# K and V loads of a decode attention kernel: the 16 key runs of a head go to its 16 partitions in the opposite order

## The chip, the core and the metric

The kernel runs on one core of a Trainium2 chip. The metric is the device time of one execution in microseconds. Before the change it is 1281.42 us (median of 3 runs, 1281.33 to 1281.44).

## The reference

One decode step for 8 sequences: a layer norm, attention over a cache of 4096 keys with 32 heads of 128, and beside it a small MLP; both are added to x.

```python
B, Sq, D = 8, 1, 640
Hq, Hkv, Sk, Dh = 32, 32, 4096, 128
...
q = (x @ wq).reshape(B, Sq, Hq, Dh).transpose(0, 2, 1, 3)
scores = einsum("bhqd,bhkd->bhqk", q, k_cache) * (Dh ** -0.5)
p = softmax(scores, axis=-1)
o = einsum("bhqk,bhkd->bhqd", p, v_cache)
A = o.transpose(0, 2, 1, 3).reshape(B, Sq, Hq * Dh) @ wo
...
out = x + A(layernorm(x)) + B(layernorm(x))     # B: layernorm, w1, gelu, w2
```

All of it is in bfloat16. K and V are 268 MB each and are read once. Softmax and the sum over keys do not depend on the order of the keys, as long as K and V have the same order.

## The kernel before

The work is cut into 32 tiles (`NQ`). Tile i holds one sequence and eight heads (`HS = 8`): K of tile i is 8 heads x 4096 keys x 128 values, 8 MiB. On chip a tile lies in `S_sb` on 128 partitions with 64 KB each: head h has partitions 16h to 16h + 15, and each partition holds a run of 256 keys (`NKEY`). In HBM the 4096 keys of a head follow each other, and so do the eight heads, so a tile is 128 runs of 64 KB, one behind the other. `cache_src` (line 364) makes this view, `load_k` (368) and `load_v` (383) load with it.

`S_sb` has three slots: two for K (tiles in turn), one for V. The loads are issued by SP in one queue, in the order K(i+1), V(i), K(i+2), V(i+1). K(i) waits for the exponentials of tile i-2 (`exp`, from tile 6 on; earlier ones for its score work), which is when its slot is free; V(i) waits until PV of tile i-1 is done. V of tile 30 comes in two loads (192 and 64 of the 256 keys). Behind K31 and V30 come the MLP's weights, then V31, then wo. x and two biases are loaded by ACT, in a queue of its own.

For each tile, once K has landed (`k_ready`):

- DVE works out the scores of 176 of each partition's 256 keys in three pieces (`dve_chunk`: multiply by the query, fold, reduce in `S_sb`).
- PE transposes the other 80, ACT copies them to `KT_sb`, PE multiplies them with the query, DVE picks each partition's own head (`dve_sel`).
- DVE finds a maximum (`dve_max`), ACT takes the exponentials (`act_exp`, into `P_sb`), PE sums them over the 16 partitions of a head (`pe_RS`).
- Once V has landed PE multiplies it with `P_sb` (`pe_PV`, 256 matmuls), ACT copies the result, POOL divides by the sum.

The engines' programs are recorded in Python, sorted by hand-set places (`at(...)`) and then replayed, so nearly every instruction carries line 111 in the profile; tiles are told apart by their names.

## Time and profile before

| | |
|---|---|
| median of 3 runs | 1281.42 us |
| profiled execution, device time | 1281.24 us |
| its span, first to last instruction | 1279.9 us |
| bytes moved | 551.97 MB |
| DVE busy | 1103.0 us (86%) |
| PE busy | 672.1 us (53%) |
| ACT busy | 476.5 us (37%) |
| POOL busy | 109.6 us (9%) |

The page cuts the span into 40 equal slices: a digit is the busy share in tenths, the DMA row is the mean share of the core's 16 DMA engines, the GB/s row what they moved. "us to landing" is the time from a load's issue to its arrival, with its wait in the queue. The chain of waits follows the end of the run back, at each step to what released it.

### The profile page before, as it was taken

Reading aid. Unit: us, or ns where it says so; the run is one execution under the profiler, and the core shown is the slowest. Engines: PE = TensorE matmul, PEld = TensorE weight load, DVE = VectorE, ACT = ScalarE, POOL = GpSimd, SP = SyncE. Lnnn points to the kernel's source line nnn. Section 1 sums busy time; section 2 is a strip of 40 time slices with the busy share of each in tenths; the row PEclk is TensorE's granted clock in tenths of the full one; section 3 lists DMA queues with packets and bytes.
Section 4 is the critical chain, followed back from the end, with each engine's and each line's share of the span. In section 5 each row is a group of like instructions: output and inputs, shape, how many; then the busy total and the mean of one; then the engine's idle time right before and its main releaser. Section 6 shows DMA issues by size and latency. Waiting matters only on the chain.

```text
span 1279.9 us, 34138 instructions
## 1 busy us (share of the span) xinstructions
PE 672.1 (53%) x13794; PEld 570.6 (45%) x13794; DVE 1103.0 (86%) x684; ACT 476.5 (37%) x906; POOL 109.6 (9%) x121
## 2 busy tenths in 40 slices
PE   2536555446645446545456554456454466464476
PEld 0435444435535345444345444345343355353465
DVE  2899998889888889888899888898888898888894
ACT  0524444233444233443234443234443334442331
POOL 0020010000000000000000000000000000000050
PEclk8656655565565556555555555555565556655665
DMA  9999999999999999999999999999999999999998
GB/s 424 425 431 429 434 434 428 440 434 430 432 438 428 438 432 432 434 432 434 430 440 430 432 434 438 428 432 436 430 438 432 432 432 440 426 434 436 426 444 365
DMA packets 10784, 551.97 MB, mean 431 GB/s; under 512 B 1242, under 2 KB 1523, under 8 KB 1812
## 3 DMA queue, kind: packets, MB, share of 16 engines
q1 hardware_dynamic: 10736, 551.79, 99.7%
q8 instruction: 8, 0.13, 0.0%
q14 instruction: 4, 0.03, 0.0%
q10 hardware_dynamic: 36, 0.02, 0.0%
HBM read 551.80 MB, written 0.01 MB: 431 GB/s over the span
## 4 chain that ended last, share of the span: by engine, by line
DMA 46%; DVE 37%; issue 12%; ACT 4%; PE 1%; DVEq 0%; SPq 0%
DMA S_sb<-in_A_k_cache_dram 42%; DVE S_sb L111 26%; DVE Sd_sb L111 8%; ACT P_sb L111 4%; DMA S_sb<-in_B_w_dram 2%; DMA S_sb<-in_A_wo_dram 2%; DVE S_ps L111 1%; PE TR_ps L111 1%; DVE mx_sb L111 1%; DVE mxT_sb L111 0%; DVE mbT_sb L111 0%; DVEq L109 0%; DVE mq_sb L111 0%; DVE NB_sb L111 0%; DVE ri_sb L111 0%
## 5 line engine op out<-in xcount | busy, mean ns | idle before, releaser
L111 PE MATMUL TR_ps<-ident_bf,S_sb 128*128 128x128 bf16 (+1 forms) x2578 | 341.8, 279 | 354.1 <-POOL kr_sb L111 331.4
L111 DVE TENSOR_TENSOR S_sb<-S_sb,qbc_sb 128x7552 bf16<-128x7552 bf16 (+1 forms) x96 | 388.8, 4050 | 127.2 <-DMA S_sb<-in_A_k_cache_dram 126.9
L111 PEld LDWEIGHTS TR_ps<-ident_bf,S_sb 128*128 (+2 forms) x2578 | 245.1, 103 | 412.4 <-issue 339.6
L111 DVE TENSOR_REDUCE Sd_sb<-S_sb 128x59 f32<-128x3776 bf16 (+1 forms) x96 | 390.2, 4065 | 6.0
L111 ACT ACTIVATE KT_sb<-TR_ps 128x1024 bf16<-128x1024 bf16 x320 | 326.6, 1023 | 120.5 <-PE TR_ps L111 109.4
L111 PE MATMUL PV_ps<-P_sb,S_sb 128*128 128x8 bf16 x8192 | 224.0, 175 | 141.3 <-DMA S_sb<-in_A_v_cache_dram 138.3
L111 PEld LDWEIGHTS PV_ps<-P_sb,S_sb 128*128 128x128 bf16 x8192 | 221.4, 103 | 144.1 <-DMA S_sb<-in_A_v_cache_dram 141.0
L111 DVE TENSOR_TENSOR S_sb<-S_sb 128x3776 bf16<-128x3776 bf16 (+1 forms) x96 | 206.5, 2151 | 3.3
L111 ACT ACTIVATE P_sb<-Sd_sb,NB_sb 128x256 bf16<-128x256 f32 x256 | 126.3, 494 | 210.1 <-DVE NB_sb L111 210.1
L111 PE MATMUL S_ps<-qrep_sb,KT_sb 128*128 128x8 bf16 x2560 | 121.9, 177 | 50.3 <-ACT KT_sb L111 47.0
L111 ACT ACTIVATE oU_sb<-PV_ps 128x8 f32<-128x8 f32 x31 | 5.5, 177 | 377.5 <-PE PV_ps L111 377.5
L111 PEld LDWEIGHTS S_ps<-qrep_sb,KT_sb 128*128 128x128 bf16 x2560 | 91.8, 103 | 82.2 <-ACT KT_sb L111 40.0
L111 POOL TENSOR_TENSOR oT_sb<-oU_sb,ri_sb 128x8 bf16<-128x8 f32 x31 | 71.5, 2306 | 371.4 <-DVE S_sb L111 315.3
L111 POOL COPY qrep_sb<-qT_sb 128x128 bf16<-128x128 bf16 x32 | 18.5, 578 | 470.0 <-PE S_ps L111 453.3
L111 ACT ACTIVATION_READ_ACCUMULATOR P_sb<-Sd_sb,NB_sb 128x1 f32 x256 | 47.7, 186 | 0.0
L111 DVE TENSOR_TENSOR S_ps<-S_ps,mask_sb 128x320 f32<-128x320 f32 (+1 forms) x65 | 31.6, 486 | 2.7 <-PE S_ps L111 2.7
L111 DVE TENSOR_REDUCE Sd_sb<-S_ps 128x40 f32<-128x320 f32 x64 | 31.5, 492 | 2.2
L111 ACT ACTIVATE qbc_sb<-QB_ps 128x128 bf16<-128x128 f32 x32 | 8.9, 277 | 58.2 <-PE QB_ps L111 58.2
L111 PE MATMUL QB_ps<-ident_bf,qrep_sb 128*128 128x128 bf16 x32 | 9.1, 283 | 40.2 <-DVE S_sb L111 21.9
L111 POOL MEMSET kr_sb<- 128x1 f32 x32 | 3.1, 98 | 295.2 <-DMA S_sb<-in_A_k_cache_dram 295.2
L111 PEld LDWEIGHTS QB_ps<-ident_bf,qrep_sb 128*128 128x128 bf16 x32 | 3.3, 103 | 43.1 <-ACT oU_sb L111 29.1
L111 PE MATMUL CH_ps<-rs_sb,ones_f 128*128 128x8 f32 x64 | 16.2, 326 | 6.1 <-ACT P_sb L111 6.1
(70 smaller groups left out, 150.1 us busy)
## 6 DMA issues: line engine op xcount, KB each, us to landing
S_sb<-in_A_v_cache_dram SPq DMA_DIRECT2D x1, 6144.0 KB, 26.8
S_sb<-in_A_wq_dram SPq DMA_DIRECT2D x1, 5120.0 KB, 15.2
S_sb<-in_A_wo_dram SPq DMA_DIRECT2D x1, 2560.0 KB, 18.4
S_sb<-in_B_w_dram SPq DMA_DIRECT2D x1, 2160.0 KB, 30.3
S_sb<-in_B_w_dram SPq DMA_DIRECT2D x1, 2080.0 KB, 34.8
S_sb<-in_A_v_cache_dram SPq DMA_DIRECT2D x1, 2048.0 KB, 31.3
S_sb<-in_A_wo_dram SPq DMA_DIRECT2D x1, 1280.0 KB, 21.1
S_sb<-in_A_wo_dram SPq DMA_DIRECT2D x1, 800.0 KB, 22.6
```

Of the source, the lines that this page charges most:

```text
L111: inst = getattr(e, name)(*a, **k)
```

## The change

`cache_src` now builds the view with head and run as separate dimensions and turns the run dimension round: partition 16h + p gets run 15 - p of head h instead of run p. It takes the range of keys as arguments, since the view has one more dimension; `load_v` passes them for tile 30. K and V use the same view, so a key's score and its value still meet in the same partition, and each partition still holds keys of its own head. The other code is as before.

```diff
-        def cache_src(cache, i):
+        def cache_src(cache, i, lo=0, hi=NKEY):
             hq, b = divmod(i, B)
-            return cache[b, hq * HS:(hq + 1) * HS].rearrange("h (p j) d -> (h p) j d", j=NKEY)
+            src = cache[b, hq * HS:(hq + 1) * HS].rearrange("h (p j) d -> h p j d", j=NKEY)
+            return src[:, ::-1, lo:hi, :]
...
-                    d.sig(sp.dma_start(tile[VS][:, lo:hi, :], cache_src(A_v_cache, i)[:, lo:hi, :])))
+                    d.sig(sp.dma_start(tile[VS][:, lo:hi, :], cache_src(A_v_cache, i, lo, hi))))
```

In the built program the source of a K load had two dimensions, 128 steps of 32768 elements with one run of 32768 each. Now it has three: 8 steps of 524288 elements (heads), 16 of -32768 (runs, backwards), and one run of 32768. PE, DVE, ACT and POOL have the same instructions in the same order. On SP, which issues the loads, the end of the program before reads as follows (K31, the two parts of V30, the weights of the MLP, V31, the first part of wo; the last numbers are the destination's shape):

```order
L111 DMA S_sb<-in_A_k_cache_dram 128x32768
L111 DMA S_sb<-in_A_v_cache_dram 128x24576
L111 DMA S_sb<-in_A_v_cache_dram 128x8192
L111 DMA S_sb<-in_B_w_dram 128x8640
L111 DMA S_sb<-in_B_w_dram 128x8320
L111 DMA S_sb<-in_B_w_dram 4x1280 x8
L111 DMA S_sb<-in_A_v_cache_dram 128x32768
L111 DMA S_sb<-in_A_wo_dram 128x10240
```

The same place after the change:

```order
L111 DMA S_sb<-in_A_k_cache_dram 128x1x32768
L111 DMA S_sb<-in_A_v_cache_dram 128x1x24576
L111 DMA S_sb<-in_A_v_cache_dram 128x1x8192
L111 DMA S_sb<-in_B_w_dram 128x8640
L111 DMA S_sb<-in_B_w_dram 128x8320
L111 DMA S_sb<-in_B_w_dram 4x1280 x8
L111 DMA S_sb<-in_A_v_cache_dram 128x1x32768
L111 DMA S_sb<-in_A_wo_dram 128x10240
```

No load has moved. The destination of a K or V load has one more dimension, of size one, to match the three of its source; the loads of the weights are as they were.

## The prediction

> **What bounds the kernel now.** I read the page's slices first, then a table of one long stretch, then the chain of waits, then the queue that issues the loads.

> ```profile
> DMA  9999999999999999999999999999999999999998
> GB/s 424 425 431 429 434 434 428 440 434 430 432 438 428 438 432 432 434 432 434 430 440 430 432 434 438 428 432 436 430 438 432 432 432 440 426 434 436 426 444 365
> DMA packets 10784, 551.97 MB, mean 431 GB/s; under 512 B 1242, under 2 KB 1523, under 8 KB 1812
> 60.00:1180.00 1120.00, 586.77 (x12122) 500.46 (x12121) 993.25 (x590) 428.41 (x827) 84.02 (x87) 0.54 1.00 434
> ```

> The DMA row has a 9 in 39 of 40 slices: the 16 DMA engines are never idle. In the stretch from 60 to 1180 us (last row: busy time of PE, PEld, DVE, ACT, POOL, then clock, DMA share, GB/s) their share is 1.00 at 434 GB/s, which is 27.1 GB/s for each of the 16. DVE is next with 993 of 1120 us. So the bytes set the time, and nothing that fills idle DMA time can be won, because there is none.

> The K and V loads are 64 times 8 MiB, 536.9 MB of the page's 552.0. At 434 GB/s a load is 8.389 MB / 434 = 19.33 us, and all of them 64 x 19.33 = 1237.0 us. The span is 1279.9 us, so 42.9 us remain for start, weights and end.

> ```profile
> 597.23 38.75 DMA S_sb<-in_A_k_cache_dram
> 635.98 0.03 issue
> ...
> 671.98 2.65 ACT P_sb L111 x11
> 674.62 0.02 issue
> 674.64 38.74 DMA S_sb<-in_A_k_cache_dram
> ```

> This is the chain in the middle of the run. A K load needs 38.75 us from issue to landing, two loads' worth (a V load is ahead of it in the queue). Its score and softmax work then takes from 635.98 to 674.64, 38.66 us, and frees the slot for the next K load. With two K slots these two pieces make two periods of 38.7 us. So DMA is full, and DVE's chain is only just fast enough.

> **What the change does, part by part.**

> *Instructions.* Nothing is added, removed or put in another order. PE, DVE, ACT and POOL do the same work on other keys of the same head. A 64-KB run is still one run and the bytes are the same.

> *How many DMA engines a load uses.* This is the term that matters. Before, a load's source has 128 equal steps: 128 rows on both sides. With the order inside a head turned round, the step from partition 15 to 16 is no longer that from 14 to 15, so the source's outer count is 8 (heads), with 16 inside; the destination keeps 128. I look in the profile for how engines are shared out, first in the window 0 to 13 us (packets, then queue q10, which carries only the two loads that ACT issues), then in 60 to 1180:

> ```profile
> DMA packets 130, 4.60 MB, mean 354 GB/s; under 512 B 9, under 2 KB 18, under 8 KB 18
> q10 hardware_dynamic: 18, 0.01, 0.3%
> S_sb<-in_A_x_dram ACTq DMA_DIRECT2D x1, 10.0 KB
> S_sb<-in_A_k_cache_dram SPq DMA_DIRECT2D x1, 34.0
> S_sb<-in_B_b_dram ACTq DMA_DIRECT2D x1, 1.2 KB
> ```

> ```profile
> DMA packets 8344, 485.60 MB, mean 434 GB/s; under 512 B 928, under 2 KB 928, under 8 KB 928
> S_sb<-in_A_k_cache_dram SPq DMA_DIRECT2D x30, 38.8
> S_sb<-in_A_v_cache_dram SPq DMA_DIRECT2D x29, 31.6
> ```

> The load of x has 8 rows and that of b2 one. Together they leave 18 packets: 9 of a row's size and 9 very short ones, so 8 + 1 short ones, one per row. In the long window 928 short packets go with 58 loads of 128 rows, 16 each. The simplest reading: every engine that takes part ends its share with one short packet, and it is 1, 8 and 16 engines for outer counts of 1, 8 and 128. With an outer count of 8 on one side, the K and V loads should get 8 engines. No load in this trace has unequal counts on its two sides, so the step from "8 rows" to "8 on one side, 128 on the other" is a choice of mine. Its bounds are 8 engines and 16; the nearest row is that of x, with 8.

> [...]

> *What 8 engines move.* Each engine brings 27.1 GB/s now. With 8 the rate is between 8/16 of the present one (each keeps its pace) and a part of that (they get in each other's way). A gain per engine is excluded on the same page rows: the share is 1.00, so they already run without a pause. The nearest row is the 434 GB/s of the same rows in the same sizes, so I take 217 GB/s: 8.389 / 217 = 38.66 us a load, 64 x 38.66 = 2474 us, 1237 more than now. Two loads do not run side by side on different halves if it is always the same 8; the window's K and V loads already take their turns in one queue (38.8 us for K is twice 19.3).

> *Order of addresses.* Each engine now reads its 64-KB runs downwards in steps. I count it at nothing, within the spread of the page's slices: 424 GB/s in the first, with rows of another length (wq), to 444 in the last but one, with the MLP's. Halved, these make the term 2418 to 2532 us.

> *Issue.* One more dimension in each load instruction may make SP slower at issuing it.

> ```profile
> 597.23 0.33 SPq L111 DMA_DIRECT2D S_sb<-in_A_k_cache_dram  x1
> 623.71 0.33 SPq L111 DMA_DIRECT2D S_sb<-in_A_v_cache_dram  x1
> 635.92 0.33 SPq L111 DMA_DIRECT2D S_sb<-in_A_k_cache_dram  x1
> L111 PE MATMUL PV_ps<-P_sb,S_sb x768: 174/175/193, 616.7 to 700.9; 128*128 128x8 bf16 x192
> ```

> An issue takes 0.33 us now, and the load then waits its turn behind another. Even at twice that, all 65 are 21 us of SP time beside the transfers; only the first K load is exposed, by 0.3 us. Counted: 0.

> *Does the queue stay full?* PV on a landed V load starts at 616.7 and the next V load goes out at 623.71, 7.0 us later. Take K(i) landing at 0 in the new pace: V(i-1) lands at 38.7, V(i) is issued at 45.7, and K(i+2), which stands behind it on SP and needs the 38.66-us chain after K(i), right after it. K(i+1) is in transit until 77.3, so both come over 31 us before the engines need them. The chain is covered with 38 us to spare, where it had none; were the cover gone, each missing us would count 32 times. At the end K31, V30, the weights and V31 follow each other in the same queue. The 42.9 us keep their length: the weights' loads have 128 rows on both sides and stay on 16 engines, so the 8 engines that also carry V move the same share of them as before.

> *Sum against the profiled execution.* 2474.1 + 42.9 = 2517.0 us of span. The execution is 1281.24 us with a span of 1279.9, so 1.3 lie outside: **2518 us**. (The median shown, 1281.42, is 0.2 above that execution.) Its own range, with 424 to 444 GB/s and a little for the start, is 2470 to 2580.

> **The rivals.**

> 1. *Engines that meet at one way into S_sb.* In the present split every engine may have partitions, and a way into them, of its own: 16 equal, constant streams fit a limit at the engines and one at 16 entrances equally well. Under the change one engine fills 16 neighbouring partitions, one after the other, and all 8 start at the first of theirs. If two of them then stand before the same entrance all the time, a pair shares what one has now: 108.5 GB/s, 77.3 us a load, 64 x 77.3 = 4948, in all **4992 us**. For it: the streams are so even (1.00, 434) that pairs which start together may stay together. Against it: no row shows two engines at one entrance, and once a pair is 4 rows apart it would no longer meet. [...]
> 2. *The same, but the pairs drift apart* after some loads. The time is then between: with x of the 64 loads at 77.3 us and the rest at 38.66, 2518 + 38.66x, for example 3755 for x = 32.
> 3. *The load keeps 16 engines* (the other side: not slower). If the counts 8 and 16 are folded to 128 before the rows are shared out, a load keeps 16 short packets and 19.33 us, and the time is 1281, with 0.33 us at most for the slower first issue. It decides at the first K load, which lands 34 us after its issue now. For it: the rows, their number and the destination's count are unchanged. Against it: x's 8 rows got only 8.
> 4. *DVE becomes the bound.* Only below 38.66 us for a pair of loads; a pair now takes 38.66 and would take 77.3. Excluded unless 3 holds.

> **How the numbers follow.** Forecast 2518 (2470 to 2580): 0.40, since it needs only the x row and the present pace. Rival 1, 4700 to 5040: 0.33, as the rows leave the place of the limit open. Rival 2, between: 0.19. Rival 3: 0.06, of it 0.05 within 0.2% (about what a measurement of this kernel can tell from no change) and 0.01 faster. Something else that is slower: 0.02. So slower is 0.94. The range runs from the forecast's low end over both rivals to 5040, 2470 to 5040, and leaves out 0.08; any cut that drops rival 1 would leave out over 0.3.

> **What would show it.** Right: 8 short packets a load (some 464 for 58 loads), half the DMA share, a steady 217 GB/s, K loads landing some 109 us after issue (46.0 to 154.6 in the count above) and V loads some 70, DVE waiting on K some 42 us in each period. Rival 1: 108 GB/s, with the share still a half, since its 8 engines are busy but slow, and K loads landing in about 225 us. Rival 2: a rate that climbs along the slices. Rival 3: 16 short packets a load and 434 GB/s. The forecast is wrong if the short packets stay at 16, or if the 8 engines move less than 27 GB/s each.

## The result, and the profile after

The changed kernel takes 5106.62 us (median of 6 runs, 5031.79 to 5129.23), the kernel before 1281.38 us in the same rounds. The ratio is 3.963 (95% interval 3.9345 to 3.9914). Its runs differ by 1.9% among themselves; the ratio leaves the three longest out, and the profiled execution, 5108.54 us with a span of 5107.2, is the shortest of these three. The forecast of 2518 us was half of it, and the range ended 67 us too low.

The page of the changed kernel, its DMA rows over 40 slices and its packets, and then one long stretch (columns as before: busy time of PE, PEld, DVE, ACT, POOL, clock, DMA share, GB/s):

```profile
DMA  5454554554455455545444545454544445445545
GB/s 136 107 109 108 108 107 106 108 108 109 111 109 111 113 110 110 111 111 112 112 108 107 105 105 106 105 106 106 107 107 108 107 104 106 104 103 106 109 87 111
DMA packets 10264, 551.97 MB, mean 108 GB/s; under 512 B 722, under 2 KB 1003, under 8 KB 1292
60.00:4600.00 4540.00, 592.93 (x12055) 504.15 (x12055) 998.19 (x586) 434.93 (x823) 25.40 (x89) 0.51 0.50 108
```

There are 722 short packets where there were 1242. The difference, 520, is 65 K and V loads times 8: each of them leaves 8 short packets, so it runs on 8 engines, no longer on 16. The share says the same, 0.50 in place of 1.00. But the rate is a quarter, 108 GB/s in place of 434: the 8 engines are busy all the time, and each brings 13.5 GB/s, not 27.1.

The single packets show how. This is the time in ns of the first 16 packets of 64 KB that one engine moves, its share of the first K load. The trace does not name a packet's engine, so the packets are put together where one starts as another ends:

```
4516 5086 5081 5085   4752 5074 5088 5084   4706 5072 5073 5084   4645 5084 5078 5081
```

In the kernel before, the median packet takes 2422 ns. Here three of each four take twice that and 5% more, 5072 to 5088 ns. The first of each four is shorter by 0.3 to 0.6 us. So the thing that slows an engine changes after each four rows.

The waits and the queue of the changed kernel (who waited for whom, in total, times, longest; then SP's issues in two periods):

```profile
DVE S_sb L111 <- DMA S_sb<-in_A_k_cache_dram: 3821.5, 32, 134.2
SPq L111 <- PE PV_ps L111: 4606.6, 31, 158.8
2134.77 0.60 SPq L111 DMA_DIRECT2D S_sb<-in_A_v_cache_dram  x1
2140.10 0.60 SPq L111 DMA_DIRECT2D S_sb<-in_A_k_cache_dram  x1
2289.64 0.60 SPq L111 DMA_DIRECT2D S_sb<-in_A_v_cache_dram  x1
2294.97 0.60 SPq L111 DMA_DIRECT2D S_sb<-in_A_k_cache_dram  x1
```

In the kernel before, the first of these rows was:

```profile
DVE S_sb L111 <- DMA S_sb<-in_A_k_cache_dram: 126.9, 28, 13.0
```

So DVE waits 3821.5 us for K, 126.9 before. A period, one K and one V load, lasts 154.9 us (2134.77 to 2289.64), 77.4 a load, where the forecast had 38.66 and rival 1 77.3. An issue takes 0.60 us, 0.33 before.

### The profile page after: what moved, and what is told of

Same layout as the page of the kernel before. It is cut to its first block, busy times and chain, and to the rows that moved or that the text cites. A ratio compares the mean times of both kernels' runs of the same rounds, so it can differ in the third digit from the quotient of the medians.

```text
span 5107.2 us, 34138 instructions
## 1 busy us (share of the span) xinstructions
PE 672.2 (13%) x13794; PEld 571.1 (11%) x13794; DVE 1103.1 (22%) x684; ACT 473.8 (9%) x906; POOL 41.8 (1%) x121
## 2 busy tenths in 40 slices
DMA packets 10264, 551.97 MB, mean 108 GB/s; under 512 B 722, under 2 KB 1003, under 8 KB 1292
## 4 chain that ended last, share of the span: by engine, by line
another core or an unknown queue 85%; PE 13%; ACT 1%; issue 1%; DMA 0%; POOL 0%; DVE 0%; ACTq 0%
PE TR_ps L111 6%; PE PV_ps L111 4%; PE S_ps L111 2%; ACT KT_sb L111 1%; DMA S_sb<-in_A_wq_dram 0%; PE CH_ps L111 0%; POOL oT_sb L111 0%; PE ACC_ps L111 0%; ACT oU_sb L111 0%; ACT P_sb L111 0%; POOL kr_sb L111 0%; DVE S_sb L111 0%; POOL qrep_sb L111 0%; PE QB_ps L111 0%
## 5 line engine op out<-in xcount | busy, mean ns | idle before, releaser
L111 DVE TENSOR_TENSOR S_sb<-S_sb,qbc_sb 128x7552 bf16<-128x7552 bf16 (+1 forms) x96 | 388.7, 4049 | 3821.5 <-DMA S_sb<-in_A_k_cache_dram 3821.5
L111 PE MATMUL TR_ps<-ident_bf,S_sb 128*128 128x128 bf16 (+1 forms) x2578 | 342.8, 275 | 2267.1 <-POOL kr_sb L111 2258.7
L111 ACT ACTIVATE KT_sb<-TR_ps 128x1024 bf16<-128x1024 bf16 x320 | 327.2, 1023 | 2224.1 <-PE TR_ps L111 2211.7
L111 PEld LDWEIGHTS TR_ps<-ident_bf,S_sb 128*128 (+2 forms) x2578 | 246.3, 103 | 2326.1 <-issue 2193.1
L111 PE MATMUL PV_ps<-P_sb,S_sb 128*128 128x8 bf16 x8192 | 224.1, 175 | 2064.9 <-DMA S_sb<-in_A_v_cache_dram 2064.9
L111 PEld LDWEIGHTS PV_ps<-P_sb,S_sb 128*128 128x128 bf16 x8192 | 221.0, 103 | 2067.8 <-DMA S_sb<-in_A_v_cache_dram 2067.8
L111 DVE TENSOR_REDUCE Sd_sb<-S_sb 128x59 f32<-128x3776 bf16 (+1 forms) x96 | 390.2, 4064 | 6.0
L111 ACT ACTIVATE oU_sb<-PV_ps 128x8 f32<-128x8 f32 x31 | 5.5, 177 | 2222.0 <-PE PV_ps L111 2222.0
L111 DVE TENSOR_TENSOR S_sb<-S_sb 128x3776 bf16<-128x3776 bf16 (+1 forms) x96 | 206.5, 2151 | 3.3
L111 ACT ACTIVATE P_sb<-Sd_sb,NB_sb 128x256 bf16<-128x256 f32 x256 | 125.9, 495 | 0.0
L111 PE MATMUL S_ps<-qrep_sb,KT_sb 128*128 128x8 bf16 x2560 | 121.6, 177 | 30.1 <-ACT KT_sb L111 26.4
L111 PEld LDWEIGHTS S_ps<-qrep_sb,KT_sb 128*128 128x128 bf16 x2560 | 91.2, 102 | 61.3 <-ACT KT_sb L111 38.6
L111 ACT ACTIVATION_READ_ACCUMULATOR P_sb<-Sd_sb,NB_sb 128x1 f32 x256 | 48.5, 190 | 0.0
L111 DVE TENSOR_TENSOR S_ps<-S_ps,mask_sb 128x320 f32<-128x320 f32 (+1 forms) x65 | 31.5, 485 | 2.7 <-PE S_ps L111 2.7
L111 DVE TENSOR_REDUCE Sd_sb<-S_ps 128x40 f32<-128x320 f32 x64 | 31.5, 491 | 2.2
L111 POOL TENSOR_TENSOR oT_sb<-oU_sb,ri_sb 128x8 bf16<-128x8 f32 x31 | 7.1, 230 | 2205.0 <-ACT oU_sb L111 2205.0
L111 POOL MEMSET kr_sb<- 128x1 f32 x32 | 3.1, 98 | 2283.6 <-DMA S_sb<-in_A_k_cache_dram 2283.6
L111 POOL COPY qrep_sb<-qT_sb 128x128 bf16<-128x128 bf16 x32 | 16.8, 526 | 449.6 <-PE S_ps L111 432.0
L111 DVE TENSOR_TENSOR oT_sb<-PV_ps,ri_sb 128x8 bf16<-128x8 f32 x1 | 0.2, 194 | 89.8 <-PE PV_ps L111 89.8
L111 PE MATMUL CH_ps<-rs_sb,ones_f 128*128 128x8 f32 x64 | 15.4, 314 | 3.6 <-ACT P_sb L111 3.6
L111 PE MATMUL QB_ps<-ident_bf,qrep_sb 128*128 128x128 bf16 x32 | 9.0, 281 | 46.1 <-POOL oT_sb L111 24.1
L111 ACT ACTIVATE qbc_sb<-QB_ps 128x128 bf16<-128x128 f32 x32 | 8.9, 277 | 65.1 <-PE QB_ps L111 65.1
```

Source lines behind the costliest of these rows:

```text
L111: inst = getattr(e, name)(*a, **k)
```

## The experiments

The theory is rival 1, "two halvings": the 8 outer steps of the source leave 8 of 16 engines, and engines whose partitions lie 32 apart fill S_sb through one way in, four partitions at a time, and halve each other's pace. The 8 engines and the step after four rows are read from the 722 short packets and the packet times above; the 32 partitions are my assumption, which the runs below test. Its opponents: the runs are read backwards ("backwards"), the eight streams, one head or 1 MiB apart, hold each other up in HBM ("memory"), or fewer engines cost more than their number for some other reason. All diffs are against the changed kernel unless a line says otherwise.

### Backwards, or memory?

`e2_forward` keeps 8 outer steps and takes every step forwards:

```diff
-            src = cache[b, hq * HS:(hq + 1) * HS].rearrange("h (p j) d -> h p j d", j=NKEY)
-            return src[:, ::-1, lo:hi, :]
+            h0 = hq // 2 * 2 * HS + hq % 2
+            src = cache[b, h0:h0 + 2 * HS - 1:2].rearrange("h (p j) d -> h p j d", j=NKEY)
+            return src[:, :, lo:hi, :]
```

> The loads keep 8 outer steps and 16 inner ones, but every step goes forwards (heads 0, 2, 4 to 14 of a group of sixteen, then 1, 3 to 15; the runs of a head in their first order). Which heads stand in a tile differs from the query's heads; the amount of work is the same. Theory 'two halvings' (8 engines, and of these two at a time fill partitions behind one way in): 108 GB/s as in the changed kernel, 4950 to 5200 us. Rival 'backwards' (8 engines at half pace because they read the runs backwards): full pace for each engine, 217 GB/s, about 2518 us. Both: 8 short packets a load, some 720 in all.

`e7_one_head` reads all eight heads of a tile from the same addresses:

```diff
-            src = cache[b, hq * HS:(hq + 1) * HS].rearrange("h (p j) d -> h p j d", j=NKEY)
-            return src[:, ::-1, lo:hi, :]
+            src = cache[b, hq * HS:hq * HS + 1].rearrange("h (p j) d -> h p j d", j=NKEY)
+            return src[:, ::-1, lo:hi, :].to_broadcast([HS, HP, hi - lo, DH])
```

> All eight heads of a tile are loaded from the tile's first head (outer step 0), the runs backwards as in the changed kernel, so seven heads of each tile see the keys of another head. The destination and its split over the engines are as in the changed kernel; the eight streams read the same addresses. Theory 'two halvings' (the loss is on the side of S_sb): 108 GB/s, 4950 to 5200 us. Rival 'memory' (streams 1 MiB apart hold each other up): the pitch is gone, so the time changes by more than 5% one way or the other: down towards 2518 if equal addresses are served together, up if they hold each other up still more.

They took 4557.84 us and 4797.52 us (one run each). Both missed the expected interval from below, and `e7_one_head` is 6.1% shorter than the changed kernel, which by the sign set beforehand (more than 5%) counts for "memory". The time is a mean over the run, so look at the rates by slices; first `e2_forward` (slices of 114 us), then `e7_one_head` (120 us):

```profile
GB/s 141 108 109 110 106 108 109 111 113 116 114 119 117 118 119 117 117 119 127 127 123 124 129 143 155 167 165 174 121 106 107 108 111 111 115 112 112 124 109 108
```

```profile
GB/s 140 105 107 107 105 105 104 106 105 106 106 105 105 105 106 105 105 106 106 107 106 107 107 109 114 119 118 120 127 125 121 113 115 126 128 134 137 159 146 126
```

Both start at the changed kernel's 104 to 110 GB/s, forwards as well as backwards and without any pitch between the streams. That speaks against "backwards" (217 from the first slice) and, for most of the run, against "memory"; the 6.1% come from the second half, where the rate rises. There it climbs in both, in `e2_forward` to 174, and falls back to 106 within two slices. The pairs seem to drift apart and to fall together again (rival 2), and the next experiments take this up.

### How the rows are shared out

Four kernels change only how many outer steps the reversal leaves. `e3_outer16` and `e10_outer32` turn round the 8 runs of each half and the 4 of each quarter of a head. `e5_outer4` and `e6_outer2` turn round the runs of two and of four heads together.

```diff
-            src = cache[b, hq * HS:(hq + 1) * HS].rearrange("h (p j) d -> h p j d", j=NKEY)
+            # e3_outer16
+            src = cache[b, hq * HS:(hq + 1) * HS].rearrange("h (a p j) d -> (h a) p j d", a=2, j=NKEY)
+            # e10_outer32
+            src = cache[b, hq * HS:(hq + 1) * HS].rearrange("h (a p j) d -> (h a) p j d", a=4, j=NKEY)
+            # e5_outer4
+            src = cache[b, hq * HS:(hq + 1) * HS].rearrange("(g h) (p j) d -> g (h p) j d", h=2, j=NKEY)
+            # e6_outer2
+            src = cache[b, hq * HS:(hq + 1) * HS].rearrange("(g h) (p j) d -> g (h p) j d", h=4, j=NKEY)
```

> Only the eight runs of each half of a head are turned round: 16 outer steps and 8 inner ones, backwards. Every theory: 16 short packets a load, some 1240 in all. Theory 'two halvings': engine e fills partitions 8e to 8e+7, so engines e and e+4 (32 partitions apart) walk through the same ways in at the same time; 16 engines at half pace, 217 GB/s, 2500 to 2650 us, with the DMA share near 1.0. Rival 'number of engines alone, with some other fixed loss': 16 engines give twice the changed kernel's rate, also about 2550, or, if the loss came with 8 engines only, about 1281. Rival 'backwards': 16 engines at half pace, about 2518. So 1281 would speak against two halvings, and 2518 against a loss that belongs to 8 engines.

> Only the four runs of each quarter of a head are turned round: 32 outer steps and 4 inner ones, backwards, with the same three dimensions in the load as in the changed kernel. An outer step is now four neighbouring partitions, the unit in which engines met in e8_lead5. 16 engines in every theory (16 short packets a load, some 1240 in all). If the rows are shared out over engines by fours as in the kernel before, no two engines meet: 434 GB/s and the kernel before's time, 1278 to 1285 us; then neither the backward steps, nor the third dimension, nor the slower issue costs anything that can be measured. If engine e gets 8 neighbouring partitions, as in e3_outer16, it gives that one's time, 2600 to 2630 us. A loss from reading backwards would show as anything between.

> The runs of each two heads are turned round together: 4 outer steps and 32 inner ones, so keys of two heads change places and the scores are those of other heads; the amount of work is the same. 4 engines, 4 short packets a load (some 460 in all); engine e fills partitions 32e to 32e+31. Two halvings: engines 0 and 1, and 2 and 3, meet all the time, 4 engines at half pace, 52 to 54 GB/s, 9900 to 10400 us, less if the pairs drift apart. Rival 'each engine keeps 27 GB/s, whatever it writes': 108 GB/s, 4990 us.

> The runs of each four heads are turned round together: 2 outer steps and 64 inner ones, with the same effect on the result as in e5_outer4. 2 engines, one on partitions 0 to 63 and one on 64 to 127. Two halvings, with a way in that is shared only 32 partitions apart: the two never meet, 2 engines at full pace, 54 GB/s, 64 x 154.6 + 43 = 9940 us, so half the engines of e5_outer4 take no longer than its four. Rival 'fewer engines cost in proportion': twice the time of e5_outer4.

| | outer steps | engines | us | GB/s |
|---|---|---|---|---|
| e10_outer32 | 32 | 16 | 1281.38 (11 runs, 1281.21 to 1281.64) | 434 |
| e3_outer16 | 16 | 16 | 2607.51 and 2625.79 | 209 |
| changed kernel | 8 | 8 | 5106.62 | 108 |
| e5_outer4 | 4 | 4 | 5434.52 (one run) | 64, then 108 |
| e6_outer2 | 2 | 2 | 9955.64 (one run) | 54 |

The rates are from these rows: of `e10_outer32` and `e3_outer16` a long stretch and the packets, of `e5_outer4` and `e6_outer2` the packets and a long stretch (of `e5_outer4` two).

```profile
60.00:1180.00 1120.00, 584.03 (x12121) 495.82 (x12118) 993.03 (x590) 428.09 (x827) 85.41 (x87) 0.57 1.00 434
DMA packets 10784, 551.97 MB, mean 431 GB/s; under 512 B 1242, under 2 KB 1523, under 8 KB 1812
```

```profile
100.00:2500.00 2400.00, 607.85 (x12562) 517.39 (x12561) 1014.00 (x600) 441.97 (x856) 23.28 (x89) 0.52 1.00 209
DMA packets 10784, 551.97 MB, mean 212 GB/s; under 512 B 1242, under 2 KB 1523, under 8 KB 1812
```

```profile
DMA packets 10004, 551.97 MB, mean 102 GB/s; under 512 B 462, under 2 KB 743, under 8 KB 1032
60.00:700.00 640.00, 44.64 (x742) 36.67 (x742) 101.59 (x60) 40.35 (x67) 4.61 (x8) 0.60 0.25 64
1300.00:5100.00 3800.00, 503.57 (x10371) 429.11 (x10372) 846.58 (x500) 361.04 (x682) 19.68 (x74) 0.51 0.25 108
```

```profile
DMA packets 9874, 551.97 MB, mean 55 GB/s; under 512 B 332, under 2 KB 613, under 8 KB 902
200.00:9500.00 9300.00, 609.35 (x12570) 518.96 (x12570) 1020.18 (x607) 442.50 (x856) 24.92 (x90) 0.51 0.13 54
```

`e10_outer32` and `e3_outer16` both have 1242 short packets, so 16 engines, both read backwards, and both have the DMA share at 1.00. One moves 434 GB/s, the other 209. The ratio of `e10_outer32` to the kernel before is 0.9999 (0.9990 to 1.0008). So what halves the rate of `e3_outer16` is neither the direction, nor the third dimension, nor the number of engines. What differs is the split into outer and inner steps, and with it, by the theory, which rows an engine gets; the trace does not show that directly. If engine e takes outer step e, then in `e3_outer16` an engine has 8 neighbouring partitions, and engine e+4 has those 32 further on. If the rows of `e10_outer32` are shared out by fours, no two engines meet; its rate says that they do not.

By the same reading `e6_outer2` has one engine on partitions 0 to 63 and one on 64 to 127. They do not hinder each other: 54 GB/s, 27 each, in the whole stretch. This also speaks against "memory": the two read 4 heads, or 4 MiB, apart, as do, by the same reading, engines 0 and 2 in `e2_forward`, whose engines bring about 13.5 GB/s each at first. `e5_outer4` has twice as many engines and starts at 64 GB/s, 16 each, by that reading with engines 0 and 1 on partitions 0 to 31 and 32 to 63. From 1300 us on it runs at 108, 27 each: by the theory its pairs have moved apart and stay apart. Both its expected times were missed. Its first stretch fits the meeting, though at 16 GB/s an engine in place of 13.5, and the second says that it is not bound to last.

### Pairs that are kept apart

In the next kernels only K of tile 0 is loaded otherwise, in three pieces, so that engines 0 to 7 get unequal shares of the first load. Which engine gets which head is the same reading as above, and that both early pieces begin at engine 0 is my assumption: no trace names an engine. The slices below are the test of both. The other loads are those of the changed kernel, with 8 engines, backwards.

```diff
             s = kslot(i)
...
+            if i == 0:
+                cut = NKEY * 5 // 16          # e4_lead: 8 // 16, e11_lead2: 2 // 16
+                for h0, h1, lo, hi in ((0, 2, 0, cut), (2, HS, 0, cut), (0, HS, cut, NKEY)):
+                    tk[("k", i)] = ld_s[s].sig(sp.dma_start(
+                        tile[s][h0 * HP:h1 * HP, lo:hi, :], cache_src(A_k_cache, i, lo, hi)[h0:h1]))
+                return
```

> As the changed kernel, with the same order of keys, but K of tile 0 comes in three loads: the first half of each run for heads 0 and 1, then for heads 2 to 7, then the second half of each run for all heads. This gives engines 0 and 1 24 rows of 64 KB (in bytes), engines 2 to 5 16 rows and engines 6 and 7 8 rows, so engine 0 stays 8 rows behind engine 2, and 4 behind 6, while the other 63 tile loads are untouched. Theory 'two halvings': two engines that meet only if they stand in the same four partitions of their 16 no longer meet, a load takes 38.7 us in place of 78, and the time falls to 2500 to 2700 us. Rivals 'backwards' and 'memory' (8 streams that read 1 MiB apart hold each other up): nothing that they speak of has changed in 63 of 64 loads; 5000 to 5150 us.

> As e4_lead, but the early parts of K of tile 0 are 80 of the 256 keys of each run in place of 128: engines 0 and 1 get 21 rows (in bytes), 2 to 5 get 16, 6 and 7 get 11. Each pair is 5 rows apart, which is past the four rows in which two engines can meet, and the most advanced engine leads by 10 rows (24 us). The next load is issued about 31 us before the last engine needs it, so no engine runs out of work; in e4_lead the lead was 16 rows (39 us), so that engines 6 and 7 ran dry and lost it. Two halvings, with a lead that only an empty queue takes away: every run stays near full pace, 2500 to 2700 us, 205 to 217 GB/s in all slices. Rival 'the phases wander by themselves': the runs differ as in e4_lead, from 2700 to 4900 us. Rival 'memory': about 5000 us.

`e9_even_split` has pieces of the same size, shared out so that no pair gets a lead:

```diff
-                for h0, h1, lo, hi in ((0, 2, 0, cut), (2, HS, 0, cut), (0, HS, cut, NKEY)):
+                for h0, h1, lo, hi in ((0, 4, 0, cut), (4, HS, 0, cut), (0, HS, cut, NKEY)):
```

> The same three pieces of K of tile 0 as e8_lead5 in size and number, but the early ones are heads 0 to 3 and heads 4 to 7, which run on engines 0 to 3 both times. Engines 0 to 3 stand 10 rows behind 4 to 7; within each pair (0 and 2, 1 and 3, 4 and 6, 5 and 7) there is no lead. Two halvings: pairs still meet, 105 to 110 GB/s for most of the run, 4700 to 5150 us. Rival 'three pieces, or any unevenness between engines, is what helped in e4_lead': 2500 to 2700 us.

> As e8_lead5 with 32 keys in place of 80: each pair is 2 rows apart, so of each four rows two are filled together (5.08 us each, as most packets of the changed kernel) and two alone (2.42 us): 15.0 us for four rows in place of 9.7. Two halvings: about 217 x 9.7 / 15.0 = 140 GB/s in the first slices after the start, and 3300 to 3900 us in all if the lead keeps or grows. Rival 'any lead at all frees the pairs': 217 GB/s and 2625 us. Rival 'the lead of e8_lead5 was not what helped': 106 GB/s and about 5000 us.

| | lead of each pair, by that reading | us |
|---|---|---|
| e9_even_split | 0 rows | 4644.36 (one run) |
| e11_lead2 | 2 rows | 4851.41 (one run) |
| e8_lead5 | 5 rows | 2624.95 (4 runs, 2623.66 to 2626.52) |
| e4_lead | 8 rows | 2692.40 and 4890.89 |

The slices of `e8_lead5` (66 us each), of `e9_even_split` (116 us), of `e11_lead2` (121 us) and of the longer run of `e4_lead` (122 us):

```profile
GB/s 205 219 216 217 217 218 219 217 216 217 217 218 219 217 216 217 217 218 217 218 217 217 217 218 217 218 217 217 216 219 217 217 218 216 217 219 217 168 124 99
```

```profile
GB/s 131 108 105 107 106 107 106 107 108 107 109 110 110 117 121 122 123 126 126 131 131 138 155 147 160 171 156 143 107 106 108 108 103 104 104 106 104 115 90 116
```

```profile
GB/s 152 119 126 132 142 151 135 135 152 138 106 104 104 105 106 104 104 104 106 105 104 105 105 105 104 105 104 105 104 104 104 104 107 104 104 104 105 107 115 121
```

```profile
GB/s 135 206 196 168 142 96 107 103 103 107 103 104 106 103 103 106 103 105 105 103 106 104 103 106 104 105 105 103 105 105 103 105 105 105 106 103 105 105 107 119
```

With a lead of five rows, set once, the 8 engines run at 217 GB/s, 27 each, up to the last slices, and the time is nearly halved, in each of 4 runs. The last three slices, 168, 124 and 99, fall below the 205 to 217 that were expected in all. Neither the addresses of the other 63 tile loads nor their split have changed. `e9_even_split` has as many pieces and a lead, but none within a pair, and starts at 105 to 108. It climbs to 171 later and falls back to 107, as `e2_forward` does, and so ends a little below the 4700 to 5150 us that were expected. So the second halving is the meeting of pairs. A lead shifts the reads of a pair in HBM as well as its writes; that the place is S_sb rests on `e7_one_head`, and on `e6_outer2` beside `e2_forward`. By `e8_lead5` the group in which they meet has at most five rows; the packets above say four. `e11_lead2` starts between the two, at 119 to 152 GB/s where 140 was expected, but the lead did not keep: after ten slices it is at 106, and the time fell outside its expected interval. `e4_lead` lost its lead too, after three slices, in one of its two runs. By the expectation of `e8_lead5` its engines 6 and 7 ran out of work. In its four stretches of 100 us from 300 to 700 us the DMA share was 0.49, 0.50, 0.47 and 0.43, and 0.50 before and after, so engines did stand idle while the lead went. Whether an empty queue takes a lead away was tried next.

`e12_one_empty`, against `e8_lead5`:

```diff
             sp.wait(tk["qmm"] if i == 0 else tk[("pv", i - 1)])
+            if i == 12:
+                sp.wait(tk[("k", i + 1)])
```

> As e8_lead5, with one more wait: before SP issues V of tile 12 (at about 1000 us) it waits until K of tile 13 has landed, so that once in the run no load is queued or in transit and all 8 engines stand idle together. Theory 'an empty queue takes the lead away' (the next load starts on all engines at once, and each pair meets from its first row on): 217 GB/s up to about 1000 us and 105 to 110 for the 38 loads behind it, 1000 + 38 x 78 + 43, about 4000 us in all, 3500 to 4150 if the pairs drift apart again on the way. Rival 'the lead stays, or comes back at once': one wait of some us, 2625 to 2680 us.

It took 3710.04 and 3717.21 us. Its slices (93 us each):

```profile
GB/s 210 217 217 217 217 217 217 216 218 217 217 105 107 107 105 105 108 108 109 110 110 115 115 117 119 124 120 127 126 133 136 134 143 147 153 156 156 161 119 101
```

One moment with no load in transit, at about 1046 us, takes the rate from 217 to 105 GB/s at once. Then it climbs over 2400 us to 161. So this empty queue ended the lead. Here the pairs then seem to drift apart slowly by themselves; in the changed kernel (103 to 113 GB/s) and in `e3_outer16` (209) they hardly do, and why was not tried. Nor was it tried why they fall together without an added wait (`e2_forward`, `e9_even_split`, `e11_lead2`). A pair that is apart works at twice the pace of one that meets, so it should run out of work early and start its next load together, but that is argued, not shown. Nor was it tried why `e8_lead5` falls off in its last three slices, where the MLP's weights come in between.

## Why the prediction was wrong

**What bounds the kernel.** Right: the DMA engines, before (a share of 1.00 at 434 GB/s) and after (DVE waits 3821.5 us for K).

**Eight engines.** Right. The choice between 8 and 16 rested on the 8 rows of x; 722 short packets, 462 with 4 outer steps and 332 with 2 bear it out. With 16 and with 32 outer steps they are 1242, as before: 2, 4, 8, 16 and 16 short packets for each of the 65 loads, and 202 others. That it is always the same 8 was an assumption, and no trace names an engine; but with a V and a K load issued 5.3 us apart (2134.77 and 2140.10) the share stays at 0.50, so two loads did not run side by side on different halves.

**What 8 engines move.** This is the step that failed: "The nearest row is the 434 GB/s of the same rows in the same sizes, so I take 217 GB/s". The row was for engines that do not meet; under the change pairs of them met and brought 13.5 GB/s each in place of 27.1. The reading that a share of 1.00 means full pace was no help: `e3_outer16` has a share of 1.00 at 209 GB/s. The same step gave the other end without a price, "a part of that (they get in each other's way)", and that was what happened. The term of 2474 us measured about 5010 (below). With the pairs apart the pace is right, 217 GB/s in `e8_lead5`; its 2624.95 us are still 107 above the forecast, and its rate falls in the last three slices.

**Order of addresses, issue.** Right at nothing: `e10_outer32` has both, with 0.53 us an issue, and keeps 1281.38 us; `e8_lead5` reads 16 runs backwards at 27 GB/s an engine.

**The queue stays full.** Right for the loads' engines in the middle of the run (the share is 0.50, half of 16). What a queue that runs empty would cost was given as the missing time alone; `e12_one_empty` shows that it costs the lead as well, some 1090 us.

**The 42.9 us.** This term was mis-sized too, though little hangs on it. It fits where no engines meet: `e6_outer2` gives 64 x 154.6 + 42.9 + 1.3, 9939 us, against 9955.64. In the changed kernel about 97 us remain: its 8064 packets of 64 KB take 4887 ns on average, 4926 us on 8 engines, which with the 84 us of the two parts of V30 makes 5010 us of the 5107.2.

**The rivals.** Rival 1 had the mechanism and nearly the price: 4992 us, 2.2% low, since two engines that meet need 5.08 us (most packets of the first K load) for two rows, not 4.84, and since what remains is 97 us, not 42.9. Its high end of 5040 left no room for that, and so the range missed. Its four rows stood on no row of the profile before; the first of each four packets, shorter by 0.3 to 0.6 us, and the 217 GB/s with a lead of five rows bear them out. That partitions 32 apart meet and those 64 apart do not was my assumption, and no trace shows it directly; the 209 GB/s of `e3_outer16`, the 217 of `e8_lead5` beside the 105 to 108 at the start of `e9_even_split`, and the 54 of `e6_outer2` fit it. I gave it 0.33 because no row showed two engines at one entrance. Rival 2 is what the rates of `e2_forward`, `e7_one_head`, `e9_even_split`, `e5_outer4` and `e12_one_empty` look like for a time; in the changed kernel it moves the rate only between 103 and 113 GB/s, the first and the last slices aside. Rival 3 is excluded by the 722 short packets.

## What to carry to other kernels

When the view of a DRAM source no longer folds to one step over all 128 partitions, look at its outer count. Here it decided how many DMA engines a load got (2, 4, 8 and 16 steps left 2, 4, 8 and 16 short packets a load, 32 steps 16) and, as the rates suggest, which partitions each of them filled. Read short packets, DMA share and GB/s together: the share halved and the rate quartered meant two losses here, not one. If an order inside a load like this one must be changed, change it in groups of four partitions: the same reversal cost a factor of four in groups of 16 (3.963), two in groups of 8 (2.0421), and nothing in groups of 4 (0.9999). The DMA share alone does not say what is moved: the same 1.00 went with 434 GB/s in `e10_outer32` and with 209 in `e3_outer16`.
